# Six PSUM banks for a convolution, two for the matrix products beside it, and a new table of slots

## The chip, the cores and the metric

The kernel runs on one core of one Trainium2 chip. The metric is the device time of one execution in microseconds (us); lower is better.

## The reference, cut to what matters

It is the gradient of a block with two branches on a normalised input `xn` (2048 x 1024): a long convolution over time done through FFTs (branch A), and a gated product with three weight matrices, 1024 x 3584 (branch B).

```python
def _A_ref(q, k, v, shift_k, ssm_k, ssm_D):
    # four-tap shift of k -> k_shift (cut)
    kv = k_shift * v
    y = irfft(rfft(kv, 2S) * rfft(ssm_k, 2S))[:S]     # written out with rfft2/irfft2
    return q * (y + kv * ssm_D)

def _B_ref(x, W_gate, W_up, W_down):
    gate = relu(x @ W_gate); up = x @ W_up
    return (gate * up) @ W_down

xn = _layernorm(A_q)
out = A_q + _A_ref(xn, ...) + _B_ref(xn, ...)
# reference(): out and the gradients of everything for grad_out (jax.vjp)
```

## The kernel before

TensorE works through the products of branch B in one long stream ("dense" products below: 128 x 128 weights, 512 columns). The convolution's short matmuls use parts of the array ("tiled") and are laid between them: a generator yields one slot after another, and after every slot comes about one dense product of 1.73 us. A slot may hold a pass on TensorE, one step for VectorE, or loads and stores. Emptying a finished PSUM tile, by ScalarE or VectorE, is called its eviction; the lead of a pass is the number of slots between the VectorE step that makes its input and the pass. R, FW, IA and RB are the constant matrices after which passes are named; `gk`, `gv` and `ghn` are gradients that the convolution stores, `y_d` a result of it that is read again later.

```python
    SLOT = 1760
    def steps(self):                               # branch A
        ...
        for gi in range(self.NG):                  # 8 groups of 128 channels, 72 slots each
            for p, d in self.slots(st, gi):
                self.run(p)                        # a pass on TensorE
                self.run(d)                        # one step on VectorE
                yield self.SLOT

    def slots(self, st, gi):                       # the table, cut
        yield f1h, tk if gi == 0 else None
        ...
        yield None, (lambda: self.gate_grad(st)) if gi == 0 else tk   # slot 3: gt = gt * xt
        yield None, tk
        yield f1g, flH                             # slot 5: first pass that reads gt
        ...
        yield self.inv_b(st, "gkv", "fCg"), qy
        yield None, qy
        yield None, start_gv                       # VectorE computes gv
        yield None, qy
        self.store_time(self.out_gv, st["cg"], st["gv"])   # its store, two slots on
```

PSUM has eight banks of 512 float32 columns. The convolution has two tiles of two banks, the dense products four of one bank:

```python
        self.ps = self.pool("a_ps", 2, space=bass.MemoryType.PSUM)            # A: tiles of two banks
        self.ps = tc.alloc_tile_pool(name="b_ps", bufs=4, space=...PSUM)      # B: tiles of one bank
```

Branch B goes through blocks of 512 columns of the weights, 24 products a block: gate, up and down for 8 strips of rows. The weights of a block, `wg` and `wu`, have one buffer each of four tiles. So the next block's loads can start only when the last gate (or up) product of this block has read the old ones, and the first gate product of the next block comes four products later.

```python
            def gate_up(sp):
                for s in (sp, sp + 1):
                    gate(s); yield from step()
                if end: load_gate()                # next block's wg, over the old one
                for s in (sp, sp + 1):
                    up(s); yield from step()
                if end: load_up()                  # next block's wu
    def col_block(self, W, fb, name, s):           # the load itself: SyncE's queue
            self.pri.pin(self.nc.sync.dma_start(out=t[:], in_=W[...]))
```

## Time and profile before

| | before |
|---|---|
| median (range) of the first 3 runs | 1914.19 us (1911.62 to 1918.26) |
| TensorE, VectorE, ScalarE busy | 99%, 48%, 32% of the span |
| TensorE idle from 98 to 676 us | 578 - 575.63 = 2.4 us |
| DMA packets under 512 B | 524,024 of 692,640 |

In SyncE's timeline (start, duration of the issue, what) of one change of block one sees why. The last gate product of the block starts its last matmul at 241.2 us, the last up product at 245.1:

```profile
237.69 1.44 SPq L96 DMA_DIRECT2D out_dram<-gk  x2
...
243.62 2.24 SPq L792 DMA_DIRECT2D wg<-in_B_W_gate_dram  x4
245.95 0.42 SPq L96 DMA_DIRECT2D out_dram<-ghn  x1
...
246.94 3.23 SPq L792 DMA_DIRECT2D wu<-in_B_W_up_dram  x4
```

`wg` is issued 2.5 us after its release, `wu` 1.9 us. Their use starts at 250.0 and 253.5, so 4.2 and 3.3 us are left between the end of the issue and the use. A transfer of such a tile takes 2.9 to 5.1 us from issue to landing in this trace, and each product starts with the first of four tiles. It is enough, with little to spare. Over all blocks after the first two the largest such lag is 3.7 us, and the smallest time left 3.2.

### The profile page before, as it was taken

To read this page: it belongs to the slowest core of one execution; us is meant where nothing else is said; L and a number is where in the kernel's file an instruction comes from. 1 tells how busy PE (TensorE), PEld (TensorE's weight loads), DVE (VectorE), ACT (ScalarE), POOL (GpSimd) and SP (SyncE) were. 2 spreads that over 40 slices of the span, in tenths; PEclk is the share of its full clock that TensorE was granted. 3 is DMA by queue.
4 is the path that set the end of the run, shared out by engine and by line. 5 is a ranking of instruction groups with operands and counts; after the bars stand their busy time and mean duration, and the time that the engine had idled before them with its cause. 6 is when DMAs were issued, how large, how long until landed. Compare 5 with 4: busy or idle time off the path is not lost.

```text
span 1912.6 us, 36039 instructions
## 1 busy us (share of the span) xinstructions
PE 1898.4 (99%) x15447; PEld 872.8 (46%) x15447; DVE 908.9 (48%) x1355; ACT 617.7 (32%) x858; POOL 15.0 (1%) x37
## 2 busy tenths in 40 slices
PE   8999999999999999999999999999999999999999
PEld 3444444444444444444444444444444544444444
DVE  6767767767767754543444444410122232222222
ACT  5854354354354344344344344311000000000000
POOL 1000000000000000000000000000000000000000
PEclk9999999999999999999999999999999999999999
DMA  9975688985784882655662633385999965555553
GB/s 244 264 190 147 171 189 185 221 191 135 182 192 134 248 232 78 171 134 183 159 172 80 174 100 122 102 244 184 255 246 239 231 159 121 121 121 121 121 121 72
DMA packets 692640, 323.13 MB, mean 169 GB/s; under 512 B 524024, under 2 KB 663040, under 8 KB 692480
## 3 DMA queue, kind: packets, MB, share of 16 engines
q1 hardware_dynamic: 681984, 299.99, 63.9%
q10 hardware_dynamic: 9216, 16.65, 2.9%
q0 software_dynamic: 1280, 4.20, 0.6%
q8 instruction: 120, 1.97, 0.4%
q14 instruction: 40, 0.33, 0.1%
HBM read 143.79 MB, written 95.44 MB: 125 GB/s over the span
## 4 chain that ended last, share of the span: by engine, by line
PE 97%; DMA 1%; DVE 1%; ACT 0%; SPq 0%; issue 0%; DVEq 0%; ACTq 0%
PE ps_x L1275 20%; PE ps_w L1048 20%; PE ps_u L799 10%; PE ps_h L799 10%; PE ps_o L1206 10%; PE ps_g L799 10%; PE ps_d L1048 9%; PE ps L72 6%; PE ps_d L1061 1%; PE ps_w L1061 1%; DMA ln_x<-in_A_q_dram 1%; DMA xt<-xn_d 0%; PE ps_r L1236 0%; DMA wu<-in_B_W_up_dram 0%; PE pst_x L831 0%; ACT ln_j L727 0%
## 5 line engine op out<-in xcount | busy, mean ns | idle before, releaser
L1048 PE MATMUL ps_w<-ugs,xn_nat 128*128 128x512 bf16 x1728 | 382.9, 379 | 0.0
L799 PEld LDWEIGHTS <-xnT 128*128 128x128 bf16 x1792 | 170.6, 98 | 214.9 <-issue 13.5
L1048 PEld LDWEIGHTS <-xn_nat 128*128 128x128 bf16 x1728 | 164.6, 98 | 200.6 <-issue 7.1
L799 PE MATMUL ps_g<-wg,xnT 128*128 128x512 bf16 x896 | 207.0, 382 | 3.9 <-DVE xnT L834 3.5
L799 PE MATMUL ps_u<-wu,xnT 128*128 128x512 bf16 x896 | 208.0, 382 | 0.2
L799 PE MATMUL ps_h<-wdT,goT 128*128 128x512 bf16 x896 | 205.6, 379 | 0.0
L1293 ACT ACTIVATE w<-xn,m 128x512 f32<-128x512 bf16 x32 | 24.3, 806 | 553.0 <-issue 317.2
L1275 PE MATMUL ps_x<-wgT,ggT 128*128 128x512 bf16 x896 | 198.6, 379 | 0.0
L1275 PE MATMUL ps_x<-wuT,guT 128*128 128x512 bf16 x896 | 198.6, 379 | 0.0
L1206 PE MATMUL ps_o<-wd,hT 128*128 128x512 bf16 (+1 forms) x896 | 187.6, 372 | 0.0
L1048 PE MATMUL ps_d<-g_nat,hs 128*128 128x512 bf16 x768 | 171.5, 379 | 0.0
L1275 PEld LDWEIGHTS <-guT 128*128 128x128 bf16 x896 | 87.7, 98 | 105.7
L1275 PEld LDWEIGHTS <-ggT 128*128 128x128 bf16 x896 | 87.7, 98 | 105.5
L1206 PEld LDWEIGHTS <-hT 128*128 128x128 bf16 x896 | 87.7, 98 | 100.0
L799 PEld LDWEIGHTS <-goT 128*128 128x128 bf16 x896 | 85.1, 98 | 104.1 <-issue 4.5
L302 DVE STREAM_TRANSPOSE flp<-C 128x1024 f32<-128x1024 f32 x48 | 90.4, 1932 | 84.9 <-ACT C L76 84.9
L902 DVE SCALAR_TENSOR_TENSOR ru<-ru,ps_u 128x512 bf16<-128x512 bf16 x112 | 76.5, 683 | 109.2 <-issue 37.1
L965 ACT CAST gh<-ps_h 128x512 bf16<-128x512 f32 x112 | 65.4, 584 | 178.4 <-PE ps_h L799 158.1
L76 ACT CAST C<-ps 128x1024 bf16<-128x1024 f32 x96 | 92.5, 1015 | 77.2 <-PE ps L72 76.3
L1152 ACT CAST wi<-ps_w 128x512 bf16<-128x512 f32 x108 | 63.8, 590 | 161.2 <-PE ps_w L1048 149.7
L1048 PEld LDWEIGHTS <-hs 128*128 128x128 bf16 x768 | 72.6, 98 | 89.5 <-issue 5.0
L1277 DVE CUSTOM_DVE_ANT_0 gx<-ps_x,gy 128x512 f32<-128x512 f32 x32 | 22.1, 691 | 182.1 <-PE ps_x L1275 182.1
(160 smaller groups left out, 1494.5 us busy)
## 6 DMA issues: line engine op xcount, KB each, us to landing
ug_d<-ru SPq DMA_DIRECT2D x112, 256.0 KB, 3.3
ugs<-ug_d SPq DMA_DIRECT2D x112, 256.0 KB, 5.1
wg<-in_B_W_gate_dram SPq DMA_DIRECT2D x56, 256.0 KB, 4.2
wu<-in_B_W_up_dram SPq DMA_DIRECT2D x56, 256.0 KB, 5.0
h_d<-ht SPq DMA_DIRECT2D x112, 128.0 KB, 2.3
hs<-h_d SPq DMA_DIRECT2D x56, 256.0 KB, 5.4
out_dram<-wi SPq DMA_DIRECT2D x56, 256.0 KB, 2.6
gt<-in_grad_out_dram SPq DMA_DIRECT2D x32, 256.0 KB, 5.0
```

The lines of the kernel that those rows point to most:

```text
L72: self.pri.pin(self.nc.tensor.matmul(out, lhsT=lhsT, rhs=rhs, start=start, stop=stop))
L76: self.pri.pin(self.nc.scalar.copy(out=out, in_=in_))
L302: self.pri.pin(self.nc.vector.transpose(out=df[:, c0:c0 + 32, :], in_=sf[:, c0:c0 + 32, :]))
L799: self.pri.pin(self.nc.tensor.matmul(ps[:], lhsT=xT[:, kt * P:(kt + 1) * P], rhs=w(kt), start=(kt == 0), stop=(kt == self.DT - 1)), always ...
L902: self.pri.pin(nc.vector.scalar_tensor_tensor(out=ru[s][:, 1, :], in0=ru[s][:, 0, :], scalar=0.0, in1=ps[:], op0=ALU.is_gt, op1=ALU.mult))
L965: self.pri.pin(nc.scalar.copy(out=gh[:], in_=ps[:]))
L1048: self.pri.pin(self.nc.tensor.matmul(ps[:], lhsT=lhsT(st), rhs=rhs(st), start=(st == 0), stop=(st == self.ST - 1)))
L1061: self.pri.pin(self.nc.tensor.matmul(ps[i][:], lhsT=lhsT(i, st), rhs=rhs(i, st), start=(st == 0), stop=(st == self.ST - 1)))
L1152: self.pri.pin(nc.scalar.copy(out=wo[0][:, d, :], in_=ps[:]))
L1206: nc.tensor.matmul(ps, lhsT=hT[:, kt, :], rhs=self.wd[:, kt, oc], start=(kt == 0), stop=(kt == self.FT - 1))
L1275: nc.tensor.matmul(ps, lhsT=T[:, kt, :], rhs=W[:, kt, oc], start=(i == 0), stop=(i == n - 1))
L1293: nc.scalar.activation(out=w[:, oc], in_=xn[:, oc], func=ACT.Identity, scale=m[:, 7:8], bias=m[:, 6:7])
```

## The change

The intent: give the convolution a third tile of two banks, so that several of its steps can run as one larger pass, with fewer changes between the tiled and the dense use of the array. The dense products keep two banks. A new table of 68 slots a group (before: 72) places the larger passes. The core of the diff, with cuts:

```diff
+        if self.taken > 2:
+            return self.xps.tile(shape, dt, name=name, tag="xps")
+        return self.ps.tile(shape, dt, name=name, tag="aps")
...
             for p, d in self.slots(st, gi):
-                self.run(p)
+                while p:
+                    self.taken, room = 0, 3 - self.held()
+                    while p and p[0][0] <= room:
+                        room -= p[0][0]
+                        p.pop(0)[1]()
...
         def start_gv():
...
-            st["gv"] = gv
+            self.store_time(self.out_gv, st["cg"], gv)
...
-        yield f1h, tk if gi == 0 else None
-        yield f1h, tk
...
+        if gi == 0:
+            yield f1h(0, 1, 2), tk
...
+            yield [], lambda: self.gate_grad(st)
+            yield f1h(3) + f1("Bg", "gt", 0, 1), None
...
+        yield ib("gkv", "fCg", 0) + ia("Cy", "Y", 0), qy
...
-        self.ps = tc.alloc_tile_pool(name="b_ps", bufs=4, space=bass.MemoryType.PSUM)
+        self.ps = tc.alloc_tile_pool(name="b_ps", bufs=2, space=bass.MemoryType.PSUM)
+        self.xps = tc.alloc_tile_pool(name="b_xps", bufs=1, space=bass.MemoryType.PSUM)
...
-        ps = [self.ps_tile(name) for _ in range(4)]
+        x = self.xps.tile([P, 2, 512], F32, name=name, tag="xps")
+        ps = [x[:, 0], x[:, 1], self.ps_tile(name)[:], self.ps_tile(name)[:]]
```

## The prediction

> **What bounds the kernel now.** I read the page's busy row first, then the chain, then TensorE's timeline, because a busy share alone cannot say whether its rate can change.
>
> ```profile
> PE 1898.4 (99%) x15447; PEld 872.8 (46%) x15447; DVE 908.9 (48%) x1355; ACT 617.7 (32%) x858; POOL 15.0 (1%) x37
> ...
> PE 97%; DMA 1%; DVE 1%; ACT 0%; SPq 0%; issue 0%; DVEq 0%; ACTq 0%
> ...
> L76 ACT CAST C<-ps 128x1024 bf16<-128x1024 f32 x96 | 92.5, 1015 | 77.2 <-PE ps L72 76.3
> ```
>
> TensorE is busy 99% of the span and is 97% of the chain that ended last; VectorE (DVE) is at half, ScalarE (ACT) at a third. So only what shortens or interrupts TensorE's stream counts. The third line is an eviction of a convolution tile from PSUM by ScalarE: about 1.02 us for each two-bank tile.
>
> In the timeline, dense products follow each other every 0.216 us (16 of ps_g start at 71.67 us, the next group at 75.13: 3.46 / 16). In between lie short convolution passes. One of them, with columns start, duration, what:
>
> ```profile
> 299.72 2.11 PE L799 MATMUL ps_g<-wg,xnT 128*128 128x512 bf16 x9
> 301.75 0.75 PE L72 MATMUL ps<-flp,FW 64*32 64x128 bf16 x64
> 302.44 1.90 PE L799 MATMUL ps_u<-wu,xnT 128*128 128x512 bf16 x8
> ```
>
> 64 small matmuls on 64x32 tiles of the array take 0.69 us, from 301.75 to 302.44. The starts of the single matmuls give the price of going in and out: last dense to first tiled is 309 ns in place of 216, last 64x128-tiled (512 columns too) to first dense is 308. So each change of tiling costs about 93 ns. The first dense matmul after it is followed after 226 ns, 10 more.
>
> TensorE also stood still once inside the convolution's stretch, in the first channel group:
>
> ```profile
> 106.63 1.03 PE L799 MATMUL ps_g<-wg,xnT 128*128 128x512 bf16 x4
> 109.80 0.61 PE L72 MATMUL ps<-gt,R 64*128 64x512 bf16 x4 [2.14 <-DVE gt L80]
> 110.33 4.88 PE L799 MATMUL ps_u<-wu,xnT 128*128 128x512 bf16 x14
> ```
>
> ```profile
> 108.00:110.00 2.00, 0.20 (x2) 0.11 (x4) 1.49 (x2) 0.29 (x1) 0.00 (x0) 1.00 0.81 254
> 110.00:114.00 4.00, 4.00 (x14) 1.32 (x11) 2.73 (x2) 1.93 (x2) 0.00 (x0) 0.57 1.05 235
> 114.00:118.00 4.00, 4.00 (x21) 1.57 (x20) 3.92 (x6) 1.93 (x2) 0.00 (x0) 1.00 0.30 53
> ```
>
> TensorE waited 2.14 us for VectorE's product gt, which itself waited 2.4 us for the load of xt. In the windows (the granted clock is the number after POOL's busy time) the clock then fell to 0.57 for some 4 us: eight matmuls at 427 ns in place of 216, 8 x 0.211 = 1.7 us more. The wait cost about 2.3 + 1.7 = 4.0 us.
>
> **What the Trainium skill says.** "TensorEngine Tiling (Array Packing)", Key Properties: "Changing tiling mode (not just tile) drains the TensorE". The trace agrees, with the 93 ns above, in and out alike. The same page, PSUM Bottleneck: tiling speeds up TensorE and not the eviction from PSUM. It agrees: 64 tiled matmuls fill two tiles in 0.69 us, and ScalarE needs 1.93 us to empty them. "TensorE: Matmul & The Clock Gate", Part 1, has the clock fall to half after an idle window of about 3.4 us; here a 2.14 us wait was enough, so that the measurement decides. "Perfetto Trace Analysis", Identifying the Most-Contended Engine, warns that matmul busy time says little of the rate; hence the pitch of starts rather than the 379 ns durations.
>
> **The change, part by part.** (1) Switches. The instruction order of both programs on TensorE holds the same 15447 matmuls. Before there are 170 tiled passes between dense work, each of one kind: 340 changes of tiling. After there are 120 passes; 50 of them hold more (22 are three FW units, 24 six R matmuls), but 52 mix two tilings (23 are RB then IA, 8 FW then IA, 7 FW then R, 7 gks then IA, 7 RB then R), so there are 120 x 2 + 52 = 292 changes. Saved: 48 x 93 ns = 4.5 us, and 50 slow first matmuls x 10 ns = 0.5 us. That an inner switch also costs 93 ns is assumed; were it free, 4.8 us more would be saved. The tiled matmuls themselves cost the same.
>
> (2) The first group. Its gate product moves from slot 4 to slot 7 of 1.73 us, its first use from slot 7 to slot 8, where one filter unit precedes it. xt landed about 108.5 us; slot 7 is about 97.7 + 0.9 + 6 x 1.73 = 109. So the wait should go, or nearly: 3.5 to 4 us saved. Everything before the first convolution pass (98 us, with the layer norm's waits) has the same order of instructions in both, so it stays.
>
> (3) Evictions. A pass now leaves up to three tiles, 3 x 1.02 = 3.05 us of ScalarE in one burst; before, two, 1.93 to 2.04. The total is unchanged. If a dense product ends just after such a pass, its eviction (0.6 us) waits until about 0.65 + 3.05 + 0.6 = 4.3 us after the pass began; its bank is needed again at pass 1.05 + 2 x 1.73 = 4.5 us. It just fits while one product lasts 1.73 us (gate, up, down); where it lasts 3.45 us it fits easily.
>
> (4) Two banks for dense products. A bank must be empty one product later, not three. Until 676 us the up products are emptied by VectorE, which works in order among the convolution's long operations:
>
> ```profile
> 292.50 0.69 DVE L902 SCALAR_TENSOR_TENSOR ru<-ru,ps_u 128x512 bf16<-128x512 bf16 x1 [0.86 <-issue]
> 293.22 0.42 DVE L904 TENSOR_TENSOR ht<-ru 128x512 bf16<-128x512 bf16 x1
> 293.56 1.94 DVE L302 STREAM_TRANSPOSE flp<-B 128x1024 f32<-128x1024 f32 x1
> 295.36 0.66 DVE L902 SCALAR_TENSOR_TENSOR ru<-ru,ps_u 128x512 bf16<-128x512 bf16 x1
> ```
>
> Here the first up eviction, its h and a 1.94 us transpose come before the second eviction, which ends at 296.02. With two banks its bank is wanted at 295.70, when the second ps_h product starts: a stall of 0.3 us that four banks hide. Setting each eviction's end in the trace against the start two products on, 8 of the 97 up products from 98 us on would stall so, by 0.02 to 0.49 us, some 2.4 us in all; no gate or down product would. In the new order 9 up evictions stand behind such a transpose (before: 9, and one behind more). Nine x 0.4 = 3.6 us, and I add 1 us for bursts of ScalarE. The new table has 68 slots for a group in place of 72, so VectorE, 74% busy from 98 to 676 us (427.9 of 578), gets denser there, about 78%.
>
> (5) Shorter leads. Some eight passes a group now follow the VectorE operation that makes their input by one slot (the last product of GKV before the second IA half, for example), where there often were two. One slot is 1.73 us, the operation 0.68, so it fits unless VectorE lags by 1 us; a tenth of the up evictions show such a lag (90th percentile 1.89 us from matmul end to eviction end, median 0.78). Four groups x 8 x 0.12 x 0.6 us = 2.3 us. Later, without VectorE evictions, hardly any.
>
> Sum: -5.0 - 4.0 + 4.6 + 2.3 = -2.1 us. Two things lean further down: inner switches may cost less, and two short waits of 1.2 us in all (near 684 us, for evictions within a four-bank product) may go. I take about 3 more for them: 1914.2 - 5 = **1909 us**.
>
> **The rivals.** (a) PSUM becomes the bound: with two banks many dense products wait for ScalarE or VectorE, and waits over 2 us drop the clock. For it: part 3's margin of 0.2 us, and VectorE's load. Against: median lags of 0.6 to 0.8 us for all three evictions, and the table keeps two slots between most passes. Say 20 waits of 1 us, a few with a clock drop: 1925 to 1935 us. (b) Nothing stalls and inner switches are cheap: 5 + 4 + 4.8 + 1.2 gives 1899 us. For it: six banks let a pass run without waiting for evictions. Against: the transposes, which do not get shorter. (c) The convolution is hidden anyway. Its DVE and ACT work is, and a convolution that ends some 26 slots (45 us) earlier gains nothing, since 47 us of dense gradient products follow it already; only its passes on TensorE count. This gives about 1914 us if waits eat the switches.
>
> **Range and chances.** The measured runs before span 1911.6 to 1918.3, so 3 us either way is noise. The gains are 9 to 15 us and well founded, the new waits 2 to 12 us and uncertain: 1902 to 1917 us. 2% is 38 us; no gain of that size exists, since all tiling changes together cost 340 x 93 ns = 32 us. Faster by over 2%: 0.01; within 2%: 0.96; slower, through rival (a) in full: 0.03.
>
> **What would show it.** Step 1: single matmul starts, 93 ns at the ends of a pass and within a mixed one; fewer convolution groups in TensorE's timeline. Step 2: no wait for gt near 110 us, and a clock near 1.00 there. Steps 3 and 4: waits of ps_h, ps_g or ps_u for VectorE or ScalarE lines L941, L935, L1004, a few tenths each, before 676 us and hardly any after. Step 5: waits of the convolution's passes for VectorE. I am wrong if TensorE's idle time from 98 to 676 us exceeds 12 us (2.4 before), if the startup moved by more than 2 us, or if evictions in bursts hold up ScalarE beyond the margin.

## More of the kernel before

Every load and store that matters here, of both branches, is issued by SyncE, in order: one that waits for its producer holds up all behind it. The dense products' own stores (`h_d`, `ug_d`) are put into that order one or two products late, so that they need not wait.

The view of TensorE's waits, with columns what waited, what ended the wait, us in total, times, longest:

```profile
PE ps_g L799 <- DVE xnT L834: 3.5, 2, 3.2
PE ps L72 <- DVE gt L80: 2.1, 1, 2.1
...
PE ps L72 <- ACT B L76: 0.9, 2, 0.5
```

No line of it names the load of a weight.

## The result and the profile after

The changed kernel takes 1943.26 us (median of 4 runs, 1940.37 to 1944.73); the kernel before took 1912.9 in the same session (4 runs, 1911.08 to 1918.26). The ratio is 1.0152, 95% interval 1.0128 to 1.0177. Ratios here and below are the mean time of one kernel's fast runs over that of the other's in the same rounds, so not quite the ratio of the medians. The change costs some 30 us, 1.5%, where 5 us of gain were predicted. The results are correct.

The busy row and the row of shares of the chain that ended last, of the changed kernel:

```profile
PE 1903.9 (98%) x15447; PEld 876.6 (45%) x15447; DVE 910.2 (47%) x1355; ACT 613.1 (32%) x858; POOL 15.0 (1%) x37
...
PE 90%; DMA 3%; DVE 3%; issue 1%; SPq 1%; ACT 1%; DVEq 0%; ACTq 0%
```

The work is the same; TensorE's part of the chain fell from 97% to 90%. TensorE's waits after the change:

```profile
PE ps_u L838 <- DMA wu<-in_B_W_up_dram: 7.5, 8, 2.4
PE ps_d L1104 <- DMA g_nat<-in_grad_out_dram: 5.7, 3, 2.9
PE ps_h L838 <- DVE ru L941: 3.3, 7, 1.7
PE ps_g L838 <- DMA wg<-in_B_W_gate_dram: 3.2, 7, 1.3
PE ps L72 <- DVE flp L310: 2.5, 4, 0.9
...
PE ps_g L838 <- ACT gh L1004: 1.6, 2, 0.8
...
PE ps L72 <- DVE gks L80: 1.4, 2, 1.2
```

The largest are for loads (`wu`, `wg`, `g_nat`): 16.4 us together, where before there was none. Waits of convolution passes for VectorE come to 5.1 us, of dense products for an eviction by ScalarE to 3.6 and by VectorE to 3.3. From 98 to 676 us TensorE idles 578 - 556.20 = 21.8 us, and 6.65 from 676 to 900 (before: 2.4 and 0.9). A wait costs 0.16 us more than its idle time, since a matmul's record lasts 379 ns and the next one would have started after 216. The granted clock fell to half near 412, 658 and 716 us, for 3.4, 3.4 and 6.8 us; before, near 35 and 110, for 3.4 us each.

Where the time went is best seen from when TensorE starts its k-th set of eight dense matmuls, of which both programs have the same 672:

| k | before, us | after, us | after minus before |
|---|---|---|---|
| 42 | 92.39 | 89.44 | -3.0 |
| 54 | 120.36 | 119.60 | -0.8 |
| 120 | 250.02 | 254.91 | +4.9 |
| 186 | 379.77 | 390.45 | +10.7 |
| 198 | 403.36 | 421.10 | +17.7 |
| 312 | 629.83 | 649.49 | +19.7 |
| 318 | 641.30 | 665.74 | +24.4 |
| 336 | 676.00 | 702.82 | +26.8 |
| 342 | 688.77 | 723.14 | +34.4 |
| 444 | 891.52 | 924.16 | +32.6 |
| 636 | 1266.60 | 1296.95 | +30.4 |

The -3.0 of the first row is not the change's doing, for profiles of kernels with the old table (5, 9 and 12 below) show it too. In this one profile of the kernel before, TensorE waited 3.18 us for `xnT` at 34 us, and the clock fell after it; in the twelve profiles of the other kernels (kernel 10 below aside) that wait is 0.4 to 2.0 us, and they come to the first convolution pass at 93.4 to 94.7 us, this one at 97.67. So the loss from 92 us on is 37 us rather than 34.

All of it is lost by 723 us. Some 3 us are convolution passes that the shorter table does earlier: at k = 342 the changed kernel has done 3,828 of their matmuls, the kernel before 3,628. They come back later. There are three steps of 5 to 8 us: near 400, 650 and 715 us, each a wait for a load with a clock drop after it. The first of them, in TensorE's timeline:

```profile
403.49 0.61 PE L838 MATMUL ps_g<-wg,xnT 128*128 128x512 bf16 x2 [0.46 <-DMA wg<-in_B_W_gate_dram]
...
412.19 4.44 PE L838 MATMUL ps_u<-wu,xnT 128*128 128x512 bf16 x12 [1.34 <-DMA wu<-in_B_W_up_dram]
```

and in SyncE's timeline of the same stretch:

```profile
392.29 1.36 SPq L96 DMA_DIRECT2D out_dram<-gk  x2
...
398.74 0.56 SPq L96 DMA_DIRECT2D out_dram<-ghn  x1
399.39 2.74 SPq L831 DMA_DIRECT2D wg<-in_B_W_gate_dram  x4
402.23 1.35 SPq L96 DMA_DIRECT2D y_d<-yt  x2
403.66 2.58 SPq L947 DMA_DIRECT2D h_d<-ht  x1
406.34 1.95 SPq L831 DMA_DIRECT2D wu<-in_B_W_up_dram  x4
```

The last matmul that read the old `wg` started at 393.7 us, the last that read the old `wu` at 398.3. So `wg` was issued 5.7 us late and `wu` 8.0 us, behind stores of the convolution: `gk`, which SyncE could issue only at 392.29 after standing idle from 388.0, then `ghn`, then `y_d`. Between the end of the issue and the use 1.4 and 1.3 us remain.

That gave the theory to test, **Q**: the new table puts convolution stores and loads into SyncE's in-order queue just ahead of the weights' loads, at places where their producers are not done or their issue takes long; the weights, with one buffer each, then come late. The rivals: **two banks** (theory **B**) and **short leads** (**L**) explain most of it (steps 4 and 5 of the prediction, under-sized), or the loads are late through **contention** among the transfers, whatever their order.

### The profile page after: what moved, and what is told of

The parts are those of the page before. It is cut to its first block, busy times and chain, and to the rows that moved or that the text cites. A ratio compares the mean times of both kernels' runs of the same rounds, so it can differ in the third digit from the quotient of the medians.

```text
span 1942.9 us, 36030 instructions
## 1 busy us (share of the span) xinstructions
PE 1903.9 (98%) x15447; PEld 876.6 (45%) x15447; DVE 910.2 (47%) x1355; ACT 613.1 (32%) x858; POOL 15.0 (1%) x37
## 4 chain that ended last, share of the span: by engine, by line
PE 90%; DMA 3%; DVE 3%; issue 1%; SPq 1%; ACT 1%; DVEq 0%; ACTq 0%
PE ps_x L1323 20%; PE ps_w L1089 19%; PE ps_o L1254 10%; PE ps_u L838 9%; PE ps_d L1089 9%; PE ps_g L838 8%; PE ps_h L838 8%; PE ps L72 6%; PE ps_d L1104 1%; DMA wu<-in_B_W_up_dram 1%; DMA wg<-in_B_W_gate_dram 1%; DVE flp L310 1%; PE ps_w L1104 1%; SPq L849 1%; DVE ru L941 0%
## 5 line engine op out<-in xcount | busy, mean ns | idle before, releaser
L1246 DVE TENSOR_TENSOR ya<-ya,xe 128x1024 bf16<-128x1024 bf16 x16 | 11.1, 693 | 223.7 <-DMA xe<-xn_d 223.7
```

## The experiments

Twelve kernels ran, all with correct results. Kernels of one session shared the runs of the kernel before, whose medians were 1914.01, 1913.7, 1913.68 and 1913.83 us. The first four share a session.

**1. Four more slots at the end of each group.** If only the place of the groups against the blocks of weights had changed (68 slots drift against 24 products a block, 72 do not), 72 slots would mend it.

```diff
         yield ibc(1), None
+        if gi:
+            for _ in range(4):
+                yield [], None
```

> The changed kernel with four empty slots at the end of every group but the first, so that a group again has 72 slots, three times the 24 products of a feed-forward block. Theory Q (the lost time is mostly weight loads that stand in SyncE's queue behind the convolution's transfers, because groups of 68 slots drift against the blocks): waits of TensorE for the loads of wg, wu and g_nat fall from 16.4 us to under 8 us, time 1925 to 1933 us. Theory B (two banks for the dense products) and theory L (inputs made one slot ahead): no change beyond 3 us, 1940 to 1946 us.

Measured: 1941.01 us (ratio 1.0141, 1.0126 to 1.0156). The waits for loads fell from 16.4 to 10.8 us, but the places where `wg` stands behind `gv` near 344 us and behind `gk` and `ghn` near 400 stayed (5.0 and 4.8 us late). Q's expectation failed, and the time is the one that B and L expected (1940 to 1946 us): 72 slots fix the relation of table and weights, but they fixed it at a bad place.

**2. The convolution's loads and stores on another queue.** Apart from the first group's loads, they are issued by GpSimd.

```diff
     def load(self, out, in_):
-        ins = self.nc.sync.dma_start(out=out, in_=in_)
+        q = self.nc.gpsimd if self.pri.strict else self.nc.sync
+        ins = q.dma_start(out=out, in_=in_)
...
     def store(self, out, in_):
-        self.pri.pin(self.nc.sync.dma_start(out=out, in_=in_))
+        self.pri.pin(self.nc.gpsimd.dma_start(out=out, in_=in_))
```

> The changed kernel with the convolution's own loads and stores, from its first group on, issued by GpSimd in place of SyncE; nothing else moved. Theory Q: waits for wg, wu and g_nat fall from 16.4 us to 3 to 5 us (what is left is the wait near 110 us, which comes before most of these transfers), the clock drops behind them go, time 1918 to 1925 us. Theories B and L: 1940 to 1946 us, with the DMA waits merely elsewhere.

Measured: 1964.35 us (1.0268, 1.0242 to 1.0293). This contradicts the expectation: waits for loads rose to 22.4 us. In SyncE's timeline nothing of the convolution stands ahead of `wg` any more, but its issue takes 9.14 us instead of 2.74:

```profile
391.01 9.14 SPq L832 DMA_DIRECT2D wg<-in_B_W_gate_dram  x4
```

In those 9 us GpSimd's queue issued `ghn`, `y_d` and `hn`. So loads of one queue are held up while a second queue, here GpSimd's, feeds transfers too. By what, this run does not show.

**3. The old table with two dense banks.** The kernel before with the new division of PSUM alone; the convolution's third tile lies idle.

```diff
-        self.ps = tc.alloc_tile_pool(name="b_ps", bufs=4, space=bass.MemoryType.PSUM)
+        self.ps = tc.alloc_tile_pool(name="b_ps", bufs=2, space=bass.MemoryType.PSUM)
+        self.xps = tc.alloc_tile_pool(name="b_xps", bufs=1, space=bass.MemoryType.PSUM)
```

> The kernel before with its old table and passes, but the dense products have two banks during the convolution; the other two are used only by the four-bank product and outside the convolution, as in the change. Theory B: many waits for evictions, 1925 us or more. Theory Q and the prediction's part 4: some 8 waits of ps_h for the vector eviction of 0.3 to 0.5 us each, 2.4 us in all, time 1913 to 1918 us, and no waits for weight loads beyond those of before.

Measured: 1921.0 us (1.0037, 1.0022 to 1.0052), so 0.0037 x 1914 = 7 us for the banks, between what Q (1913 to 1918 us) and B (1925 or more) expected. Its waits have no load of a weight:

```profile
PE ps_h L805 <- DVE ru L908: 3.3, 7, 1.9
...
PE ps_w L1054 <- DVE so L84: 1.5, 1, 1.5
```

Against the kernel before, TensorE's progress falls back by 2.9 us between 122 and 667 us, and by another 3.3 after that, at evictions by ScalarE (`wo`) and VectorE (`so`) in the part where products last 3.45 us. The second half was predicted to be nearly free.

**4. Four more slots, each where a lead is short.** As in 1 the groups have 72 slots, but the empty ones stand ahead of the passes that follow their VectorE input closely.

```diff
+        if gi:
+            yield [], None
         yield f2("H", "fH", 3) + f2("G", "fG", 0, 1), tk     # and ahead of three other passes
```

> The changed kernel with the same four added slots for each later group, but one each ahead of the mixed H/G pass, of the first K pass, of the first gkv pass and of the halo, where TensorE waited for VectorE's flips, Y and gks. Theory Q: 1925 to 1933 us as with the slots at the end. Theory L adds: the waits for flp, Y, gks and gt (some 5 us with their clock) fall below 1.5 us, so 3 to 4 us faster than with the slots at the end. Theory L alone would give 1937 to 1940 us.

Measured: 1927.63 us (1.0072, 1.0057 to 1.0087), 13 us under kernel 1 with the same number of slots. Waits of convolution passes for VectorE are 3.9 us (5.1 after the change, 6.5 in kernel 1), waits for loads 7.2. So Q's range held, but L had expected the waits for VectorE below 1.5 us. Slots at these places lower both kinds of wait: `wg` near 343 and 391 us is now issued 0.5 us before and 0.6 us after its release, where kernel 1 had 5.0 and 4.8 us. How the 13 us divide is not shown; kernel 1's trace also has four stretches of half clock (3.4 us each) and this one none. Three loads of `wu` are still late, two behind `gv` (3.7 us each) and one behind `gk` (4.4).

**5. The wait for gt alone.** The kernel before, with the first group's two passes that read `gt` moved from slots 5 and 7 to 7 and 8. (The text counts from one further on; the edit is this.)

```diff
-        yield f1g, flH
+        yield None if gi == 0 else f1g, flH
         yield None, flH
         yield f1g, tk
-        yield next_1, tk
+        yield self.both(f1g, next_1) if gi == 0 else next_1, tk
```

> The kernel before, with one thing of the change: in the first group of convolution work the two passes that read gt stand at slots 8 and 9 instead of 6 and 8, so that TensorE doesn't come to them before gt is computed. Step 2 of the prediction (the 2.14 us wait for gt and the clock drop behind it are saved): 1909 to 1911 us against about 1914, and no new wait in the stretch from 97 to 112 us. The masked theory (the schedule of the loads fixes when wu lands, near 110 us, and the wait for gt only hid that): the wait for gt goes, a wait of 1.5 to 3 us for wu appears at about 107 to 110 us, and the time stays within 1 us of the kernel before.

Measured: 1914.47 us (ratio 1.0001, 0.9988 to 1.0014). The wait for `gt` is gone. In its place TensorE waits for weights:

```profile
103.34 5.58 PE L799 MATMUL ps_g<-wg,xnT 128*128 128x512 bf16 x16 [2.47 <-DMA wg<-in_B_W_gate_dram]
109.26 1.32 PE L799 MATMUL ps_u<-wu,xnT 128*128 128x512 bf16 x4 [0.34 <-DMA wu<-in_B_W_up_dram]
```

By 122 us the kernel is 0.7 us ahead of the profiled run of the kernel before, at the end 0.1. It had been 3.7 us ahead at the first convolution pass (the wait for `xnT`, see above), so the weights, issued at 97.8 and 103.3 us here and at 97.3 and 102.5 before, took back that lead too. So the gain that step 2 counted does not exist; the masked theory holds, though the larger new wait is for `wg` and not, as expected, for `wu`.

**6. Four stores later.** The changed kernel; `gv` is stored three slots later, `gk` two, `y_d` and `ghn` at the next group's third slot.

```diff
-            self.store_time(self.out_gv, st["cg"], gv)
+            st["gv"] = gv                       # stored three slots on
...
+        def late_stores(st):                    # run in the next group's third slot
...
-        self.store_time(self.out_gk, st["cg"], gk)
         yield ibc(1), None
...
         yield [], None
+        self.store_time(self.out_gk, st["cg"], gk)
```

> The changed kernel with four of the convolution's stores issued later, behind their producers: the gv store three slots later, the gk store two, the y_d and gh stores at the next group's third slot. Nothing else moves. Theory Q (the weights' loads wait in SyncE's in-order queue behind a store whose producer is not done): TensorE's waits for weight loads fall from 16.4 us to 8 or 9 (those at the startup, behind the kp load at 643 us and at 714 us stay), the loads of wg and wu near 201, 343, 399 and 402 us are issued under 3 us after they could be, and the time is 1931 to 1936 us. Rival (the loads are slow because of the amount of fine-grained traffic itself, whatever the order of the queue): waits for weights stay within 3 us of 16.4 and the time at 1939 to 1945.

Measured: 1936.18 us (1.0118, 1.0103 to 1.0134), 7 us less than the changed kernel and just above the upper edge of what Q expected (1936 us). In SyncE's timeline of the change of block near 390 us `y_d` and `ghn` now come behind the weights, and `gk` no longer waits:

```profile
389.50 1.40 SPq L96 DMA_DIRECT2D out_dram<-gk  x2
391.01 3.40 SPq L838 DMA_DIRECT2D wg<-in_B_W_gate_dram  x4
...
395.01 2.01 SPq L838 DMA_DIRECT2D wu<-in_B_W_up_dram  x4
```

The time from a buffer's release (start of the last matmul that reads it) to the start of the issue, at the five late places:

| load, about | changed kernel | behind | stores later |
|---|---|---|---|
| wu, 200 us | 3.7 us | gv | 0.4 us |
| wg, 343 us | 5.0 us | gv | -0.4 us |
| wg, 394 us | 5.7 us | gk, ghn | 1.6 us |
| wu, 398 us | 8.0 us | ghn, y_d | 1.0 us |
| wu, 646 us | 6.6 us | kp, vt, skb | 7.1 us |

(A small negative value: the first of the four tiles is free before the last matmul starts.) The first four are mended and TensorE's waits there are gone. The fifth stands behind loads of `kp` that were not moved, and its wait stayed:

```profile
PE ps_d L1111 <- DMA g_nat<-in_grad_out_dram: 4.5, 3, 2.3
...
PE ps_u L845 <- DMA wu<-in_B_W_up_dram: 4.4, 4, 2.6
```

All waits for loads together fell from 16.4 to 9.4 us; Q had expected 8 or 9, the rival over 13. A store that is moved takes its traffic along, so this edit does not wholly part the order of the queue from contention. For the order speaks that the changed kernel's loads of `wu`, once issued, land no later than before (median 3.8 us, before 5.0).

**7. Both: more slots at the leads, and later stores.** Kernel 4 with the stores of kernel 6.

> The kernel of pads_at_leads (the changed table with four empty slots added in each later group, ahead of passes with short leads) with the same four stores issued later. Theory Q: its remaining waits for weights, 7.2 us, fall to 3 or 4 and the time from 1927.6 to 1922 to 1925 us. Rival (the traffic itself): waits stay near 7 and the time at 1926 to 1929.

Measured: 1921.2 us (1.0036, 1.0020 to 1.0051), as Q expected or a little better. From 120 us on no weight is issued over 1.1 us after its release, and the waits for loads are 2.5 us, all at the start of the convolution. The new table, cleared of both, is as slow as the old one with two banks (1921.0).

**8. Each division of PSUM where it might pay.** The old table, with three dense tiles in turn, for the first four groups; the new one for the last four.

```diff
+        if gi < self.SPLIT:                     # 4: the old table
+            yield from self.slots_two(st, gi, ...)
+            return
```

> A version meant to beat both: the first four groups of convolution work follow the table of the kernel before, with four PSUM banks for the convolution and three tiles in turn for the matrix products; the last four groups, which run beside the weight-gradient products of 3.45 us each, follow the new table with six banks and two. Theory (the switches saved are worth 93 ns each, and two dense banks, short leads and late weight loads cost only where products are short and are evicted by VectorE and ScalarE in turn): no wait for a weight load in the first half, 1909 to 1912 us, 2 to 5 us under the kernel before. Rival (in the second half too, the new table's short leads take back what the switches save): 1913 to 1918 us, with over 3 us of waits in the convolution's passes after 700 us.

Measured: 1915.64 us (1.0004, 0.9992 to 1.0017), no gain; the rival is nearer. The first half was not free of waits for weights: 4.6 us, nearly all at the start of the convolution. Still, progress against the kernel before is level at 687 us, and 1.5 us behind at the end. In the second half there is a wait of 0.7 us for an eviction (`wo`), and one of 1.54 us in the middle of an IA pass, at 876 us, for which the profile names no releaser. The rival had put over 3 us there, so the cost is only in part where it said. What the switches save there is not seen in the time.

**9. The load of xt behind wu.** To find what holds the start of the convolution, the kernel before with the first group's `xt` issued behind `wu`, and the passes that need it later.

```diff
-        self.load_xn(nx)                        # ahead of the first slot
...
+            yield lambda: self.load_xn(st), self.both(lambda: self.add_D(st), tk)   # slot 2
```

> The kernel before with the first group's load of xt issued behind the loads of wu instead of ahead of them, and the work that needs it (gt, and the two passes that read gt) three or four slots later; same number of slots. Theory (the start of the convolution is set by when wg and wu land; 1.5 us of SyncE's time for xt stands ahead of wu): wu's wait near 110 us, 1.9 us in before_gt_later, goes; wg's of 2.5 us at 103 us stays, since nothing ahead of it moved; 1911 to 1913 us, against about 1914. Rival (the loads contend at the transfer engines and not in the queue, or something else sets the start): the wait for wu stays within 0.7 us and the time within 1 us of the kernel before.

Measured: 1913.75 us (1.0000, 0.9987 to 1.0013): no gain. `wu` was issued from 101.72 us instead of 102.52, and its wait fell only to 1.4 us; `wg` was waited for 2.1 us, and a filter pass, which I had moved forward, 1.4 us for VectorE. The rival, that something else than `xt` sets the start, stands.

**10. The first group's loads on GpSimd's queue.** Kernel 9, with `hn`, `gt`, `sD`, `kp` and `vt` of the first group issued by GpSimd.

```diff
+        self.first = True
         nx = self.loads_1(0)
         self.loads_2(nx)
+        self.first = False                      # load(): gpsimd while first, else sync
```

> xt_later, with the first group's loads of hn, gt, sD, kp and vt (13.5 us of SyncE's time between 73 and 88 us in the kernel before) issued by GpSimd's queue. They are then issued earlier, and no dense store stands behind them in SyncE's queue. Theory: the stores of ug_d and h_d go out in time, wg is issued at its buffers' release near 92 us instead of 97 us, and the wait for it goes too: 1908 to 1911 us, no wait for a weight load over 1 us between 90 and 115 us. Rival (as in conv_pool_queue, fine-grained transfers from a second queue slow the others): waits for other loads appear between 10 and 90 us, and the time is 1913 or more.

Measured: 1932.86 us (1.0105, 1.0083 to 1.0127). A miss: GpSimd issues these loads from 10 us on, among the loads of the start, and TensorE waited 25.2 us for `goT`, a load of the dense products, at 51.7 us. It says nothing on the start at 97 us, but once more that loads from a second queue at the wrong time cost much.

**11 and 12. The weights alone on their own queue.** The cleanest test of waiting in the queue: `wg` and `wu` go through GpSimd, which has nothing else to do; all else stays. Kernel 11 is the changed kernel with this edit, kernel 12 the kernel before.

```diff
+        self.blocks += 1
+        queue = self.nc.sync if self.blocks <= 4 else self.nc.gpsimd
...
-            self.pri.pin(self.nc.sync.dma_start(out=t[:], in_=W[...]))
+            self.pri.pin(queue.dma_start(out=t[:], in_=W[...]))
...
-        nc.gpsimd.memset(kp[0:1, 0:3, :], 0.0)
+        self.pri.pin(nc.vector.memset(kp[0:1, 0:3, :], 0.0))
```

> The changed kernel with wg and wu, from the third block of each on, loaded through GpSimd's queue, which has nothing else to do then; the small memset of kp moves from GpSimd to VectorE so that nothing stands ahead of them there. The table, the banks and every other transfer stay. Theory Q (these loads come late because they stand behind convolution stores in SyncE's in-order queue): they are issued within 1 us of their buffers' release, the waits for wg and wu (10.7 us of the 16.4) fall under 2 us, and with the clock drops behind them the time falls by 10 to 14 us, to 1929 to 1933; the waits for VectorE and ScalarE and for g_nat stay, about 18 us. Rival (they are late because of contention among the transfers themselves): they are issued at once but take 5 us and more to issue and land, the waits stay over 7 us, and the time is 1938 or more.

> The kernel before with the same one thing done: wg and wu of the third and later blocks through GpSimd's queue. It was not short of weights except at the start of the convolution work, where wg and wu landed near 103 and 110 us. Theory Q: there they are issued at their buffers' release, 4 to 5 us sooner, the wait shrinks to that for gt or less, nothing changes later: 1909 to 1913 us against 1914. Rival (contention): weights land as late or later, and waits for them appear in the steady part as well: 1914 to 1925.

Measured: 1949.5 us (1.0180, 1.0165 to 1.0196) and 1924.83 us (1.0054, 1.0040 to 1.0067). Q's expectation failed in both, and the rival's, contention, was met (1938 us or more, and 1914 to 1925): the weights are issued at once, and come later still. An example of kernel 11, from the timelines of GpSimd, SyncE and TensorE, one line each:

```profile
350.00 2.82 POOL L833 DMA_DIRECT2D wu<-in_B_W_up_dram  x4 [1.19 <-PE ps_u L840]
```

```profile
355.15 12.71 SPq L857 DMA_TRANSPOSE goT<-in_grad_out_dram  x2
```

```profile
364.20 5.34 PE L840 MATMUL ps_u<-wu,xnT 128*128 128x512 bf16 x16 [4.12 <-DMA wu<-in_B_W_up_dram]
```

`wu` is issued at 350.00, the moment the last up product releases its buffer, and the issue ends at 352.82; TensorE gets it at 364.20. SyncE's two transposing loads take 12.71 us to issue in the meantime; in the changed kernel the same two took 4.91. The windows of this stretch (start and end, length, then busy time of TensorE, its weight loads, VectorE, ScalarE, GpSimd, then clock, busy share of the transfer engines, GB/s):

```profile
350.00:354.00 4.00, 3.78 (x18) 1.62 (x17) 3.93 (x6) 0.59 (x1) 2.82 (x4) 1.00 1.16 302
...
355.00:358.00 3.00, 3.00 (x132) 1.91 (x131) 3.00 (x6) 1.04 (x2) 0.00 (x0) 1.00 0.77 51
358.00:363.00 5.00, 2.08 (x38) 0.81 (x22) 1.13 (x3) 2.46 (x3) 0.00 (x0) 1.00 1.08 82
```

The two queues did not just share the rate there: the rate of all transfers fell from 302 to 51 and 82 GB/s. In the changed kernel, while the same two loads are issued, it is 343 (353.5 to 356 us) and 217 (356 to 358.4). Whether a transposing load beside any second queue does this, or GpSimd's way of issuing, no run here separates: the second queue was always GpSimd's.

The view of the tile `wu` from 98 to 680 us gives the time from issue to landing, first for the changed kernel, then for kernel 11:

```profile
DMA to landing us min/median/max: 3.6/3.8/5.5
```

```profile
DMA to landing us min/median/max: 3.3/5.3/14.2
```

This limits the theory rather than overturning it. In the changed kernel the transfers land as fast as before (before: 2.9 / 5.0 / 5.1 us); there the lateness is in the issue, and kernel 6 mends four of its five places by moving stores. But a queue of their own is no cure: taking the waiting away by GpSimd's queue costs more than the waiting did. The Trainium skill has both halves on its page "DMA: Bandwidth & Descriptors". In Anatomy of one DMA (told there of GpSimd's path): "DMA engines do not wait on semaphores", the wait happens on the issuing engine before dispatch; the trace agrees, for SyncE's queue, since SyncE stands idle from 388.0 to 392.29 us ahead of `gk`. In Issuing engines are not separate DMA queues: transfers of all issuing engines run on the same 16 DMA engines and interleave; 14.2 us in place of 5.5 fits that, but sharing alone does not explain the fall to 51 GB/s.

## Why the prediction was wrong, by its steps

Two steps of the sum failed: step 2, whose 4 us of gain did not come, and the sum as a whole, which had no term for loads that come late; these are the largest part of the loss. In steps 3 to 5 the waits that were named came, and were longer than foreseen.

**Step 1, switches: the price is right, the sum is seen only in part.** A change inside a mixed pass costs as much as one at its ends: from an RB matmul to an IA one the starts lie 309 ns apart, after a matmul of 216. So the saving of 5 us rests on counted changes times a measured price; no experiment isolates it, and kernel 8, which should have shown half of it, did not in its time. The traces that hold all 15,447 matmuls allow a sum: over all passes, from the last dense start before to the first one after, less 216 ns and less the waits, it is 140.4 to 140.7 us in four kernels with the old table and 137.2 and 138.0 in two with the new. So about 3 us were saved, and the waits ate them.

**Step 2, the wait for gt: failed.** The wait went, as said (0.4 us left, and a clock of 1.00 from 100 to 120 us in place of 0.91). The 4 us did not come, because `wg` and `wu` landed no earlier: SyncE issued them at 97.3 and 102.5 us before, at 97.5 and 102.4 after. (The text puts the old table's first use of `gt` at slot 7; in its own count it is slot 6.) Kernel 5 shows the replacement of one wait by the other at no change in time. The "wait that takes the place of the one removed" was among the questions, and I had not asked it of this wait.

**Step 3, bursts of evictions: size off.** Step 3 found that they just fit, and step 4 allowed 1 us for them. Dense products wait 3.6 us for ScalarE in the changed kernel, in five waits of up to 0.9 us, and before not at all. Four of the five, 2.9 us, fall on the short products (up to 703 us), where the margin was 0.2 us; that a burst causes each of them is not shown.

**Step 4, two banks: mechanism right, size off.** Predicted 4.6 us, nearly all before 676 us; kernel 3 measures 7, of which some 3.3 come after it. The stalls of `ps_h` behind VectorE's eviction of the up product are the ones described, 7 of them, 3.3 us; but one of 1.9 us, at the start of the convolution, makes up more than half, where 0.49 us was the longest foreseen.

**Step 5, short leads: mechanism right, size off.** Predicted 2.3 us; convolution passes wait 5.1 us for VectorE. The term took the lag of evictions in the old table as the chance of a late operation. That the new table's 68 slots leave less room may add to it, but is not shown: kernel 1, with 72 slots, has 6.5 us.

**The term left out.** Nothing in the sum was for loads, and they are the largest part: 16.4 us of waits in 18 places, 18 x 0.16 = 2.9 us more, and the clock drops near 412, 658 and 716 us (13.7 us at half clock in all, before 6.8; at half speed, an estimate of 3.4 us more lost). The page before did not warn of it: no wait named a load. The lag and the time left would have: 3.7 us at worst and 3.2 us left, so nothing for a table that moves stores. That `gv`'s store was now ordered in its producer's slot stood in the diff. For four of the five late places kernel 6 shows this cause. For `wu` at 646 us and `g_nat` at 714 the queue shows loads ahead (`kp` with 6.12 us of issue; `hn` and `gt`), and with the slots of kernels 4 and 7 these waits go, but for 0.9 us for `g_nat` in kernel 4; they were not mended one by one.

Rival (a), which I gave 1925 to 1935 us, had the right direction and the wrong cause. My own sign of failure, over 12 us of idle time from 98 to 676 us, was met with 21.8. The sign of a startup moved by over 2 us was met in number too (3.0), but by the wait for `xnT` in the profile of the kernel before.

The parts, as the experiments measure them: later stores take off 7 us, slots at the leads 16, both 22, which leaves 1921.2; two banks cost 7. What stays open is how the remainder above the kernel before divides in kernel 7 between banks, start and leads, and how much of the 3 us of switches that the traces show reaches the time. No version here beats the kernel before; the nearest, kernels 5, 8 and 9, equal it.

## What to carry to other kernels

When a change moves loads and stores in program order, look at the issuing engine's queue as at any engine: for each load into a single buffer, the time from release to issue, what stands ahead of it, and the time left until its use. A store belongs into an in-order queue when its producer is done, and behind a load that is about to be needed. Before counting a wait as saved, ask what would have been waited for had it not been there; and do not expect a second queue to cure a late load without a trial: in all four kernels that used GpSimd's queue as one, loads came later.

## What the Trainium skill lacked or had wrong

- "DMA: Bandwidth & Descriptors", Issuing engines are not separate DMA queues, says that issuing on several engines at once saves only the time to initiate. That section does not say that it can cost: the same loads of `wu` landed in up to 14.2 us (median 5.3) from GpSimd's queue and in up to 5.5 (median 3.8) from SyncE's, and the kernel before lost 0.5% by it. How much of this is GpSimd's way of issuing is not separated here.
- The same page says where a wait for a semaphore takes place, but has no word on what it does to a load behind a store whose producer is late. Here `wg` and `wu` were issued up to 8.0 us after their buffers' release, behind such stores.
- The same page does not give how long an issue lasts when the transfers are busy: four loads of `wg` took 2.74 us of SyncE's time in one kernel and 9.14 in another, two transposing loads 12.71.
- "TensorEngine Tiling (Array Packing)", Key Properties, names the drain at a change of tiling without a price: 93 ns here, in, out, and between two tilings (309 ns in place of 216).
- "TensorE: Matmul & The Clock Gate", Part 1, has, in its table of the two states, the clock fall after an idle window of about 3.4 us (further on it tells, without a length, of frequent short idling): here it fell after a wait of 2.14 us (near 110 us, before), and after waits of 0.40 and 1.34 us within 3 us of each other (near 412 us, after).
